# One list reordered: packed attention and an ELU network, with GpSimd's waits for VectorE counted when the list was made

## The chip, the cores and the metric

The kernel runs on one core of a Trainium2 chip. The metric is the time of one execution on the device in microseconds (us), the median of several runs. The engines are named as in the profile: PE is TensorE (matmuls; PEld its weight loads), DVE is VectorE, ACT is ScalarE, POOL is GpSimd, SP is SyncE, which issues the DMAs.

## The reference

Eight batches of eight heads; the queries, keys and values have 576 positions of 64 elements, and there are 32 packing queries `p` for each head. All is float32.

```python
def sm_attn(qq, kk, vv):                 # scale = 1/8
    s = scale * np.matmul(qq, kk.transpose(0, 1, 3, 2))
    s = s - np.max(s, axis=-1, keepdims=True)
    a = np.exp(s)
    a = a / (np.sum(a, axis=-1, keepdims=True) + 1e-09)
    return np.matmul(a, vv)
p_packed = sm_attn(p, k, v)
out = sm_attn(q, p_packed, p_packed)     # [8, 8, 576, 64]
x = out.transpose(0, 2, 1, 3).reshape(4608, 512)
h = x @ w_in                             # [4608, 2048]
g = np.where(h > 0.0, h, np.exp(np.minimum(h, 0.0)) - 1.0)
return g @ w_out                         # [4608, 512]
```

## The kernel before

**Attention.** For each batch the packing attention gives `ppT`, 32 packed rows for each head. The second attention's weights `a` are a [256, 576] matrix for the batch (8 heads times 32 packs, in two groups of 128), made on DVE by transposes, reductions and subtractions (lines 900 to 948) and one exponential on ACT. `ppT` times `w_in` gives a matrix `m`, so that `h` is `a` times `m` over 256 rows (line 1272, in the first two batches 1543).

**Precision.** A matmul runs on parts: each operand is split into a high part (a cast on ACT, line 434) and a low part (word minus high part, on DVE or POOL), and three products (high by high, high by low, low by high) are summed in PSUM.

**The hidden layer.** Its 16 tiles of 128 columns are taken one after the other. In the first two batches each tile goes through two ACT instructions (1561, 1567), the ELU on DVE (1570), the cast (434), the low part `sub_own` (1585, DVE or POOL) and the output matmuls (1658 to 1661). From batch 2 on two tiles go together through a seven-product scheme: after the ELU (1279) three sums of blocks, of 128, 256 and 128 columns, are made in place in a tile `w8` (or `kvq`, for the 64 leftover rows of several batches), each on POOL or on DVE (1354); then one cast of 896 columns on ACT (`hi`, 434), one subtraction on DVE (`lo`, 1362), and 42 matmuls into four PSUM banks (1426). At the end of a visit (16 tiles of one batch) DVE adds the four banks up (1458), and the next visit's matmuls wait for these banks.

**The order.** No scheduler decides it. Some 3,400 operations are recorded, each with the engines it may run on; then the string `ORDER` is read, number by number, and each operation is emitted. A letter behind a number (V, A, G) names DVE, ACT or POOL; without one the first engine of the operation's list is used. `PLACES` gives the PSUM bank of each operation that takes one, `ONES` the matmuls on ones that are put behind some operations at the start. Each engine runs its own instructions in the order emitted, and so does SP's DMA queue.

**GpSimd and VectorE.** Operations that read two tensors of SBUF, and casts and scalings there, are marked `two`. When one of them is emitted on POOL, it gets a wait for the last `two` operation that was emitted on DVE, whether it uses its data or not:

```python
if o.two and e in ("DVE", "POOL"):
    made = nc.cur_bb.bb.instructions[at:]
    if e == "DVE":
        last_two = made[-1]
    elif last_two is not None:
        tc.add_manual_dep(made[0], last_two.name, ...)
```

So the place of a POOL operation in `ORDER`, not its data alone, says when it may start.

Of the kernel before, what the change touches and what calls it, by code (L numbers as in the profile page):

```python
# [25 lines left out]
2 1 7 0 8 9 11 416 417A 418 403 404A 405 10 14 12 3 4 406V 407G 15A 16V 17 18A 19A 20 21 13 23V 408  # L26
22V 409V 410 24 25A 5 26 27 28 29 400 401A 30 402 529 530A 31 424 32 33 34 6 37 425A 426 419 48 55
49 50 420A 755 756 762 757 38 763 421 35A 764 758 39 765 759A 422V 766A 56 40 41 531 57 42 532A 769
43 760G 761 59 411 412A 413 58 62 440 441A 442 767G 60 65 61 414A 63A 64A 432 433V 434 36 770 771
772 776 66A 67A 533 534 773A 44 51 777 778 52 68 69A 415G 535 435 436A 774G 783 784 45 768 70A 71  # L30
779 780V 785 72A 423V 781V 790 427 786 787V 437 438V 428A 429 557 791 792 793 788G 551 552 553 775
558 456 457A 430A 53 439V 801 802 803 458 559 431G 73 74 75 794A 795G 809 76 443 444A 448 810 449A
804 811 445 446A 450 447G 812 805 77 814 782 789 78 554 79 80 560 555 561 562 806A 818 826 54 95
807G 796 815A 816G 81 808 46A 817 459 460A 47 556 819 820 821 822 827 797A 536 828 829 84 82A 461
799A 83 831 823A 451 835 843 452A 453 824G 825 813 85 86 87 832A 462A 833G 834 537 836 837 839 538
830 838 102 844 88 845 848 463G 846 89 90 91 840A 841G 849A 850V 92 852 472 473A 454A 455G 853 854
855 96 856 504 860 861 862 865 863 842 851 93A 94 97 103 857A 491 858V 866A 867V 505A 474 873 880
874 875 492A 506 876 877A 104 878V 859 493 881 800 882 883 887 105 847 499 868 864 884V 500V 885V
888 889 894 890 895 896 897 399 891A 892V 98 501 494A 483 879 464 901 908 798 898A 899V 495V 886 893
902 903 904 475 484A 485 465A 466 909 910 905A 906V 911 502A 503V 871A 915 916 106 917 918 467 900  # L40
922 912A 907 913G 468A 919V 933 486A 469 920V 487V 914 872 923 921 924 925 488 476A 470A 477 478V
496 934 935 937 936 480 926V 489A 515 927V 941 950 107 938A 479V 939V 490 942 943 946 928 940 951
952 954 523 944 953 497A 498 947A 955A 948G 481A 109 958 482 967 956G 959 960 961 945 471G 520 963
968 949 964V 969 516A 970 971 965G 929A 975 507 976 111 957 977 517 978 980 521A 931A 522 972A 981V
973V 984 524A 518A 962 982V 525 985 519V 526V 986 987 563 564 988 992 993 994 508A 565 979 995 966
974 983 989A 997 998A 509 1001 1009 999V 512 112 513A 566 990V 514 991 510A 511V 110 1000 527G 528
1002 643V 932 1003 644V 1005 1004 1006V 1022 567 1010 1011 1012 1014 568 1015A 1016V 1029 996 869A
1007G 1008 1017 113 99 1023 1024 1030 1031 645V 1025 1026V 646A 649V 654A 1032 1033A 652V 653V 655V
930 1034V 108 870 545 569 1018A 1019 1027V 1042 1049 546 547 1020A 1043 1050 1051 1044 1028 650G
# [24 lines left out]
585 1340 586 1326 1327 1328 1350V 1377 1351G 1362 1354 1355 1363 1364 1341 1352 1365V 1366V 1367V
1368 163 1353 1369 1378 1379 1380 1342 1343 1393 1394 1381V 1382G 1395 1396 1397V 1344 1357 1398G
1358 1359 1356 1360 1383V 1384 1399V 1385 1400 1401 1409 1432 1410 1411 1433 165 1434 146 1370 1371
1373 1374 1375 166 167 1412 168 1372 1386 1376 161 169V 1435 1437 1438 1413G 1439 1414G 1415V 1416
1436 1442 1387 1389 1390 1440 1388 1402 1455 170A 1460 1443V 171 1456 1457 1417 1444V 1391 1459 1458
1392 1405 172V 1461 1478 1403 1404 1418 147 148 1462 1463 1465 1445G 1296 1446 1447 173 174 1441 175
176 1479 1483 1480 1481 1406 1484 1466G 1482 1407 1485 1488 1486 177 178 179 1408 1421 1293 1425A  # L80
1489V 195 1467G 1468G 1469 1464 1419 1420 1448 1449 1501 1506 1502 1470 1426 1507 1422 1423 1424
1451 1503 1505 1508 1504 1509 1511 1524 1487 1490G 1491G 1529 1427 1428 1429 196 1492 1493 184 1525
1510 1430 1530 1452 1450 1453 1454 1531 1474 1471 1512G 1513V 1526 1527 1532 1528 1534 180 181 185
1514G 1472 1515 1516 1535G 1536G 1537G 1547 1548 1549 1475 1473 1494 1495 1550 1552 1553 1554 1551
1476 1477 1497 1496 186 187 1557 1533 1555 1570 1538 1571 1539 1558G 1559G 1517 1518 1519 1540 1560G
1572 1574 587 588 589 1575 1576 1577 1573 1578 1498 1499 1580 1500 188 189 1579 1556 190 191 1520
1521 202 1593 1541 1598 1581G 1522 1523 192 1561 1594 1595 1596 1582G 1583G 182A 1562 183 1597 1543
590 1544 1542 1599 1600 1603 1431 1545 1546 1563 1584 193A 591 1601 1564 1566 194 1585 1623 1628 592
1567 1624 1625 1626 1629 1630 1604V 1605V 1606V 1627 1607 593 594 1631 1565 1568 1569 1646 1586 1589
1602 1633 1634G 1635G 1608 1647 1648 1649 595 1587 1651 1652 1653 1650 1590 1588 1609 1591 197 1592  # L90
1656 1657V 1658G 1610 203 206 1632 1611 1639 1654 1640 1641 207 210 204 1636G 1637 208 1638 211 1612
209 1613 1616A 1617 1618 1619 1662 1663 1614 1659G 198 1669 1670 1671 1672 1674 1675 1615 1664 1685
1686 205 1655 1620 1621 1622 1676 1677 1678 1660 1673 1679 212 199 1661 1642 1643 1680V 1644 1645
215 213 1692 1693 1697 216 1665 1681G 1682V 1666 1667 1694 217 218 1698 1695 1683 1696 1699 1702
1687 1700 214 1684 1708 1715 1709 1703G 1716 1717 1720 1701 219 1704V 1705V 1718 596 1668 1688 1721
# [108 lines left out]
ONES = {0: 3, 8: 10, 17: 2, 21: 3, 24: 2, 26: 13, 529: 5}  # L204
# [1606 lines left out]
```

## Time and profile before

| | us |
|---|---|
| three runs, median (lowest, highest) | 686.59 (686.38, 689.18) |
| the profiled execution, its own time | 687.01 |
| its span, first to last instruction | 685.2 |
| PE busy | 642.9 |
| DVE busy | 532.1 |
| ACT busy | 421.1 |
| POOL busy | 173.9 |

The span is one execution as the profiler recorded it; an engine's busy time is the union of its instructions. Matmuls overlap each other in the record, so a busy PE is not a PE at its peak; idle time of PE is time in which it had nothing in flight.

### The profile page before, as it was taken

What the parts mean: (1) busy time and instruction counts of PE and PEld (TensorE: products, weight loads), DVE (VectorE), ACT (ScalarE), POOL (GpSimd) and SP (SyncE); (2) the same over time, 40 slices, a digit from 0 to 9 for tenths busy, and PEclk for the clock granted to TensorE, in tenths of its full rate; (3) what the DMA queues carried; (4) which work ended last, traced back from release to release, by engine and by line L of the source; (5) the groups of instructions that cost most, each with busy time, mean ns of one, the idle gap of its engine ahead of it and who ended that gap; (6) DMA issues with size and microseconds to landing.
All of it is one profiled execution on the core that took longest, in us unless ns stands there. A gap on an engine that the chain in (4) does not pass through costs nothing. (4 is left out here: it accounts for less than half of the span.)

```text
span 685.2 us, 16414 instructions
## 1 busy us (share of the span) xinstructions
PE 642.9 (94%) x6125; PEld 565.0 (82%) x6125; DVE 532.1 (78%) x1068; ACT 421.1 (61%) x804; POOL 173.9 (25%) x275
## 2 busy tenths in 40 slices
PE   8898999998999899999999889998999999999995
PEld 3567987787789788888999788988788888999895
DVE  3998998686998788768888688777877788558465
ACT  3687996555777577645676477645465656445341
POOL 1133023523232242122322232221122322221420
PEclk9999999999999999999999999999999999999998
DMA  9966775654689769887589778877794765574562
GB/s 341 363 219 219 281 208 169 216 170 158 214 277 313 232 212 308 270 286 272 173 264 332 217 235 287 284 247 235 231 345 130 227 211 170 169 228 146 177 194 77
DMA packets 103711, 159.41 MB, mean 233 GB/s; under 512 B 26192, under 2 KB 43088, under 8 KB 103504
## 3 DMA queue, kind: packets, MB, share of 16 engines
q1 hardware_dynamic: 103344, 157.84, 70.7%
q8 instruction: 48, 0.79, 0.5%
q10 hardware_dynamic: 288, 0.52, 0.2%
q14 instruction: 31, 0.25, 0.1%
HBM read 131.85 MB, written 26.48 MB: 231 GB/s over the span
## 5 line engine op out<-in xcount | busy, mean ns | idle before, releaser
L1354 POOL TENSOR_TENSOR w<-w 128x128 f32<-128x128 f32 (+1 forms) x178 | 103.1, 581 | 304.7 <-DVE g L1362 96.4
L434 ACT CAST g<-w 128x896 fp32r<-128x896 f32 x96 | 89.7, 939 | 103.9 <-POOL w L1354 79.2
L1426 PE MATMUL psum<-sw,g 128*128 128x256 f32 x1008 | 150.8, 277 | 1.5 <-DVE part L1458 1.5
L1362 DVE TENSOR_TENSOR g<-w,g 128x896 fp32r<-128x896 f32 x96 | 104.9, 1095 | 47.7 <-ACT g L434 47.0
L1426 PEld LDWEIGHTS psum<-sw,g 128*128 128x128 f32 x1008 | 131.4, 192 | 7.3 <-issue 3.5
L1272 PE MATMUL psum<-a_hi,m_hi 128*128 128x256 f32 (+1 forms) x384 | 113.5, 296 | 9.7 <-DVE w L1279 5.9
L1272 PE MATMUL psum<-a_lo,m_hi 128*128 128x256 f32 (+1 forms) x384 | 110.7, 288 | 0.4 <-DVE a_lo L948 0.4
L1272 PE MATMUL psum<-a_hi,m_lo 128*128 128x256 f32 (+1 forms) x384 | 110.6, 288 | 0.0
L1426 PE MATMUL psum<-wo_a,g 128*128 128x256 f32 x672 | 95.8, 279 | 9.1 <-DVE part L1458 5.1
L1426 PE MATMUL psum<-wo_b,g 128*128 128x256 f32 x672 | 95.6, 277 | 2.1 <-DVE g L1362 2.0
L1426 PEld LDWEIGHTS psum<-wo_a,g 128*128 128x128 f32 x672 | 85.0, 193 | 15.0 <-ACT e L1287 3.4
L1426 PEld LDWEIGHTS psum<-wo_b,g 128*128 128x128 f32 x672 | 84.7, 192 | 6.7 <-issue 3.5
L1272 PEld LDWEIGHTS psum<-a_hi,m_hi 128*128 128x128 f32 x384 | 73.5, 191 | 19.2 <-issue 7.2
L1272 PEld LDWEIGHTS psum<-a_lo,m_hi 128*128 128x128 f32 x384 | 73.6, 192 | 0.6 <-DVE a_lo L948 0.6
L1272 PEld LDWEIGHTS psum<-a_hi,m_lo 128*128 128x128 f32 x384 | 73.5, 191 | 0.0
L1284 ACT ACTIVATE e<-psum 128x320 f32<-128x320 f32 x96 | 41.1, 432 | 33.6 <-PE psum L1272 29.5
L1287 ACT ACTIVATE e<-e 128x320 f32<-128x320 f32 x96 | 44.5, 470 | 2.5
L1354 DVE TENSOR_TENSOR w<-w 128x128 f32<-128x128 f32 (+1 forms) x110 | 37.6, 346 | 9.5 <-POOL w L1354 7.3
L1279 DVE SCALAR_TENSOR_TENSOR w<-e,psum 128x256 f32<-128x256 f32 x96 | 38.7, 415 | 7.5 <-ACT e L1287 6.7
L1024 DVE TENSOR_TENSOR m_lo<-psum,m_hi 128x1024 fp32r<-128x1024 f32 (+1 forms) x38 | 38.7, 1022 | 2.8 <-ACT m_hi L434 2.5
L1279 DVE SCALAR_TENSOR_TENSOR w<-w,psum 128x512 f32<-128x512 f32 x48 | 32.6, 681 | 10.4 <-ACT w L1287 9.6
L1284 ACT ACTIVATE w<-psum 128x512 f32<-128x512 f32 x48 | 28.6, 597 | 19.0 <-PE psum L1272 10.2
(135 smaller groups left out, 1160.4 us busy)
## 6 DMA issues: line engine op xcount, KB each, us to landing
sw<-sw_dram SPq DMA_DIRECT2D x288, 256.0 KB, 4.2
kvq<-in_v SPq DMA_DIRECT2D x16, 512.0 KB, 4.5
raw<-in_w_in SPq DMA_DIRECT2D x16, 511.8 KB, 5.6
raw<-in_w_out SPq DMA_DIRECT2D x16, 511.8 KB, 5.5
kvq<-in_kT SPq DMA_DIRECT2D x14, 576.0 KB, 5.5
kvq<-in_qT SPq DMA_DIRECT2D x14, 576.0 KB, 6.0
out<-part SPq DMA_DIRECT2D x28, 256.0 KB, 4.2
sw_dram<-sw SPq DMA_DIRECT2D x24, 256.0 KB, 2.7
```

The lines of the kernel that those rows point to most:

```text
L434: (nc.scalar.copy if e == "ACT" else nc.vector.tensor_copy)(out=out, in_=in_)
L1024: nc.vector.tensor_tensor(out=m_b[1].t[:, :, fs], in0=ps.t[:, :, :w], in1=m_b[0].t[:, :, fs].bitcast(F32), op=ALU.subtract,)
L1272: nc.tensor.matmul(ps, lhsT=m_b[p].t[:, g, o:o + P], rhs=in_turn(st.a.t[q][:, g, cols]), start=(n == 0), stop=(n == 3 * G - 1),)
L1279: nc.vector.scalar_tensor_tensor(out=out, in0=e_, scalar=-1.0, in1=ps, op0=ALU.add, op1=ALU.max)
L1284: nc.scalar.activation(out=out, in_=ps, func=AF.Relu, scale=-1.0)
L1287: nc.scalar.activation(out=x, in_=x, func=AF.Exp, scale=-1.0)
L1354: eng(e).tensor_tensor(out=out, in0=x, in1=y, op=o)
L1362: nc.vector.tensor_tensor(out=g_b.all[:, 7 * P:(7 + b1 - b0) * P], in0=blocks(b0, b1), in1=g_b.all[:, :(b1 - b0) * P].bitcast(F32), op=ALU ...
L1426: nc.tensor.matmul(a.t[:, at * H:(at + rhs.shape[1]) * H], lhsT=operand(blk, p), rhs=rhs, start=new and n == k == 0, stop=a.final == (u, m ...
```

## The change

The recorded operations are the same, with the same code. `ORDER`, `PLACES` and `ONES` are new: every operation may stand in another place, on another of its engines and in another bank. Line numbers are one lower after the change. The rule of waits above is unchanged. Of the diff two pairs of lines stand here: the place in `ORDER` around operation 841, a `sub_own`, and `ONES`.

```diff
--- before.py
+++ after.py
-830 838 102 844 88 845 848 463G 846 89 90 91 840A 841G 849A 850V 92 852 472 473A 454A 455G 853 854
+838 839 88 89 843 844 845 846 847 453 825 848 834 505A 840A 849V 841V 90 91 850V 454A 455G 852 853
...
-ONES = {0: 3, 8: 10, 17: 2, 21: 3, 24: 2, 26: 13, 529: 5}
+ONES = {0: 3, 8: 8, 17: 2, 21: 6, 24: 2, 26: 13, 529: 4, 37: 1}
```

Counted over the whole list, 32 of the 141 short block sums on POOL and 4 of the 64 long ones go to DVE, and 5 of 30 `sub_own`; 6 casts of `g`, 5 high parts of weights and two of `a` go from ACT to DVE; a few weight operations change in both directions. POOL has 268 instructions of the list before and 230 after, DVE 1,066 and 1,120, ACT 786 and 770.

**First place.** VectorE before, in the second batch; `sm2` and `tmp` belong to a softmax (L922 to L942), `e`, `hb` and `g` to the hidden layer.

```order
L1570 SCALAR_TENSOR_TENSOR e_826<-e_826,psum_101 128x256 [waits Activation_49,Pool_49]
L1570 SCALAR_TENSOR_TENSOR hb_823<-e_826,psum_101 128x64
L922 TENSOR_REDUCE sm2_833<-tmp_758 128x18 [waits DVE_49]
L925 TENSOR_SCALAR sm2_833<-sm2_833 128x18 [waits DVE_49]
L928 RECIPROCAL sm2_833<-sm2_833 128x18 [waits DVE_49]
L931 TENSOR_TENSOR tmp_758<-tmp_758,sm2_833 128x576 [waits DVE_49]
L1585 TENSOR_TENSOR g_841<-e_826,g_841 128x256 [waits Activation_49]
L942 STREAM_TRANSPOSE tmp_844<-tmp_758 128x576 [waits DVE_49]
```

Operation 841 (`g_838<-e_817`) is not in these rows: it stands on POOL and, by its place in the list, waits for the row L931.

VectorE after, same place; the tiles `g_838` and `e_817` are now numbered `g_849` and `e_812`.

```order
L921 TENSOR_REDUCE sm2_820<-tmp_741 128x18 [waits Activation_49]
L1569 SCALAR_TENSOR_TENSOR hb_816<-e_828,psum_101 128x64 [waits Activation_49]
L482 SCALAR_TENSOR_TENSOR mi_833<-raw_681,tops_120 128x512 [waits DMAHW1_49]
L1569 SCALAR_TENSOR_TENSOR e_828<-e_828,psum_101 128x256
L433 CAST g_851<-e_828 128x256 [waits DVE_49,PE_49]
L1584 TENSOR_TENSOR g_849<-e_812,g_849 128x256 [waits Activation_49]
L924 TENSOR_SCALAR sm2_820<-sm2_820 128x18
L927 RECIPROCAL sm2_820<-sm2_820 128x18 [waits DVE_49]
L930 TENSOR_TENSOR tmp_741<-tmp_741,sm2_820 128x576 [waits DVE_49]
L1584 TENSOR_TENSOR g_851<-e_828,g_851 128x256
```

Operation 841 is now on DVE (`g_849<-e_812`) and stands ahead of the softmax's rows L924 to L930.

**Second place.** GpSimd before, some 229 us into the run; each `w8` tile gets three block sums, here those of two pairs that follow each other.

```order
L1354 TENSOR_TENSOR w8_2981<-w8_2981 128x128 [waits DVE_49,Activation_49]
L1354 TENSOR_TENSOR w8_2981<-w8_2981 128x256 [waits DVE_49,Pool_49]
L1354 TENSOR_TENSOR w8_2981<-w8_2981 128x128 [waits Pool_49]
L1354 TENSOR_TENSOR w8_3055<-w8_3055 128x256 [waits DVE_49]
L1354 TENSOR_TENSOR w8_3055<-w8_3055 128x128 [waits Pool_49]
```

The second sum of `w8_2981` has a wait for DVE.

VectorE before, same place; `sm2` and `tmp` are a softmax's, `hb` and `w8` rows L1279 are ELUs, L1362 is `lo`, L1458 adds up the banks of a visit that has ended.

```order
L1279 SCALAR_TENSOR_TENSOR hb_3044<-e_3035,psum_101 128x64 [waits DMAHW0_49,Activation_49]
L1279 SCALAR_TENSOR_TENSOR w8_3055<-e_3035,psum_101 128x256
L1279 SCALAR_TENSOR_TENSOR w8_3055<-e_3052,psum_101 128x256 [waits Activation_49]
L1279 SCALAR_TENSOR_TENSOR hb_3044<-e_3052,psum_101 128x64
L922 TENSOR_REDUCE sm2_3067<-tmp_3021 128x18 [waits Activation_49]
L925 TENSOR_SCALAR sm2_3067<-sm2_3067 128x18 [waits DVE_49]
L928 RECIPROCAL sm2_3067<-sm2_3067 128x18 [waits DVE_49]
L1354 TENSOR_TENSOR w8_3055<-w8_3055 128x128
L1362 TENSOR_TENSOR g_3087<-w8_2981,g_3087 128x896 [waits PE_49,Activation_49]
L1458 TENSOR_TENSOR part_85<-part_85,psum_101 128x256 [waits DMAHW7_49,PE_49]
```

That wait is for the row L1354 of `w8_3055`, a sum of the next pair, which stands behind seven other rows, none of them of `w8_2981`.

GpSimd after; `w8_2981` is now `w8_2995`, `w8_3055` is `w8_3098`.

```order
L1353 TENSOR_TENSOR w8_2995<-w8_2995 128x128 [waits DVE_49]
L1353 TENSOR_TENSOR w8_2995<-w8_2995 128x256 [waits Pool_49]
L1353 TENSOR_TENSOR w8_2995<-w8_2995 128x128 [waits DVE_49,Pool_49]
L1353 TENSOR_TENSOR w8_3098<-w8_3098 128x128 [waits DVE_49]
L1353 TENSOR_TENSOR w8_3098<-w8_3098 128x256 [waits DVE_49,Pool_49]
```

The second sum has no wait for DVE left, and the next pair's first sum is now on POOL as well.

VectorE after, from the ELUs of `w8_2995` on.

```order
L1361 TENSOR_TENSOR g_2969<-w8_2886,g_2969 128x896 [waits PE_49,Activation_49]
L1278 SCALAR_TENSOR_TENSOR w8_2995<-e_2986,psum_101 128x256 [waits DVE_49,Activation_49]
L1278 SCALAR_TENSOR_TENSOR hb_3000<-e_2986,psum_101 128x64 [waits DMAHW2_49]
L1278 SCALAR_TENSOR_TENSOR w8_2995<-e_3002,psum_101 128x256 [waits Activation_49]
L1278 SCALAR_TENSOR_TENSOR hb_3000<-e_3002,psum_101 128x64
L899 STREAM_TRANSPOSE tmp_3017<-psum_101 128x576 [waits DMAHW5_49,DMAHW4_49,DMAHW6_49,DMAHW3_49,PE_49]
L908 TENSOR_REDUCE mx2_3039<-tmp_3017 128x18 [waits DVE_49]
L911 TENSOR_TENSOR tmp_3017<-tmp_3017,mx2_3039 128x576 [waits DVE_49]
L1361 TENSOR_TENSOR g_3012<-w8_2946,g_3012 128x896 [waits Activation_49]
L1278 SCALAR_TENSOR_TENSOR hb_3095<-e_3047,psum_101 128x64 [waits DMAHW0_49,Activation_49]
```

The first sum's wait is for the last ELU row of `w8_2995` (L1278), and no sum of the next pair stands between the two.

## Rows read from the trace of the kernel before

**Rows 1.** The page, part 1: span; busy time, share, instructions of each engine.

```profile
span 685.2 us, 16414 instructions
...
PE 642.9 (94%) x6125; PEld 565.0 (82%) x6125; DVE 532.1 (78%) x1068; ACT 421.1 (61%) x804; POOL 173.9 (25%) x275
```

**Rows 2.** PE waits: who ended them, us in total, times, longest.

```profile
PE psum L1426 <- DVE part L1458: 6.6, 6, 2.0
PE psum L1272 <- DVE w L1279: 5.9, 6, 2.4
PE psum L1661 <- POOL g L1585: 5.0, 4, 1.8
...
PE psum L1536 <- ACT m_hi L434: 2.0, 1, 2.0
```

**Rows 3.** Waits of the other engines, same columns.

```profile
POOL w L1354 <- DVE g L1362: 96.4, 35, 8.1
ACT g L434 <- POOL w L1354: 79.2, 38, 5.5
...
DVE g L1362 <- ACT g L434: 60.7, 52, 2.9
POOL w L1354 <- DVE w L1354: 50.0, 25, 8.0
```

**Rows 4.** Timeline 60 to 65.2: start, us, instruction; idle before, its releaser.

```profile
62.73 0.76 DVE L931 TENSOR_TENSOR tmp<-tmp,sm 128x576 f32<-128x576 f32 x1
...
63.65 0.75 POOL L1585 TENSOR_TENSOR g<-e,g 128x256 fp32r<-128x256 f32 x1 [2.45 <-DVE tmp L931]
...
64.46 0.70 PE L1661 MATMUL psum<-wo_a,g 128*128 128x512 f32 x2 [1.75 <-POOL g L1585]
```

**Rows 5.** Timeline 226 to 234.5, same columns.

```profile
229.11 0.23 DVE L1354 TENSOR_TENSOR w<-w 128x128 f32<-128x128 f32 x1
...
229.48 1.26 POOL L1354 TENSOR_TENSOR w<-w 128x256 f32<-128x256 f32 x2 [1.79 <-DVE w L1354]
...
230.78 0.94 ACT L434 CAST g<-w 128x896 fp32r<-128x896 f32 x1 [2.39 <-POOL w L1354]
...
231.75 1.09 DVE L1362 TENSOR_TENSOR g<-w,g 128x896 fp32r<-128x896 f32 x1 [2.41 <-ACT g L434]
...
232.76 0.41 DVE L1458 TENSOR_TENSOR part<-part,psum 128x256 f32<-128x256 f32 x1
...
233.32 0.91 PE L1426 MATMUL psum<-wo_a,g 128*128 128x256 f32 x6 [2.03 <-DVE part L1458]
```

**Rows 6.** Timeline 672 to 674.5, PE alone.

```profile
673.26 0.71 PE L1426 MATMUL psum<-wo_b,g 128*128 128x256 f32 x4 [0.42 <-DVE g L1362]
```

**Rows 7.** Groups by form: busy us, mean ns; idle before, its releasers.

```profile
L1354 POOL TENSOR_TENSOR w<-w 128x128 f32<-128x128 f32 x121 | 58.5, 485 | 234.2 <-DVE g L1362 73.3 <-DVE w L1279 72.8 <-DVE w L1354 30.5
...
L1354 DVE TENSOR_TENSOR w<-w 128x128 f32<-128x128 f32 x71 | 20.9, 298 | 3.7 <-POOL w L1354 2.1
...
L1354 DVE TENSOR_TENSOR w<-w 128x256 f32<-128x256 f32 x39 | 16.9, 432 | 5.7 <-POOL w L1354 5.2
...
L1585 DVE TENSOR_TENSOR g<-e,g 128x256 fp32r<-128x256 f32 x34 | 14.1, 430 | 1.3 <-ACT g L434 1.2
...
L434 DVE CAST g<-e 128x256 fp32r<-128x256 f32 x15 | 5.4, 369 | 0.8
```

**Rows 8.** Stretches of 50 us: PE, PEld, DVE, ACT, POOL busy; clock; DMA.

```profile
50.00:100.00 50.00, 48.25 (x337) 41.59 (x337) 45.08 (x99) 43.51 (x96) 10.80 (x13) 1.00 0.69 229
...
150.00:200.00 50.00, 47.27 (x354) 38.76 (x353) 43.13 (x96) 32.75 (x76) 14.92 (x20) 1.00 0.63 210
```

**Rows 9.** Source line L1354 on DVE: duration ns min/median/max.

```profile
L1354 DVE TENSOR_TENSOR w<-w x110: 228/293/840, 193.2 to 670.1; 128x128 f32<-128x128 f32 x71, 128x256 f32<-128x256 f32 x39
```

**Rows 10.** Two stretches at a PE gap, columns as in Rows 8.

```profile
546.00:550.00 4.00, 2.02 (x18) 1.86 (x17) 3.29 (x8) 3.11 (x6) 0.73 (x1) 1.00 0.18 65
550.00:553.00 3.00, 3.00 (x17) 3.00 (x17) 2.90 (x6) 0.91 (x2) 0.00 (x0) 0.61 0.10 22
```

More of the change, by code (lines that the diff above doesn't have):

```diff
@@ L194 @@
[L194 to L195 removed]
+2 1 7 0 8 9 10 11 403 404V 12 405 406V 407V 3 14 15A 16A 17 4 416 417V 418 400 5 20 18A 19A 13 21
+401V 22A 23A 408 24 424 402 25A 26 27 28 29 6 48 55 49 409A 410 529 30 530A 425A 419 31 32 33 34 37
+50 426 35A 755 38 39 36 756 757 758 40 762 763 764 765 56 420A 421 759A 766V 760G 57 531 59 41 767V
+532A 769 58 776 411 62 412V 60 65 413 422A 61 414V 432 761 433A 434 415V 440 441A 442 770 777 771
@@ new lines @@
+977 524A 980 978 979 525 981V 966 521A 522 985 986 982V 987 988 508A 992 993 994 509 510V 512 995
+997 974 989A 990V 526A 929V 527V 998A 999V 1001 1009 1002 1003 1005 511V 98 99 996 1004 513A 1010
+1011 514 528 1012 983 991 112 1006A 1007V 643V 1014 1022 930 1023 1024 113 931A 932 566 567 1000
+1008 644V 645V 1015A 1016V 646A 1025 1026A 568 114 1029 647V 649V 654A 652V 1027V 1030 1031 653V
+1017 1018A 1042 650V 1028 655V 656 1020A 1021 1032 1033A 545 657V 658G 569 1043 1044 1045 1046A 1049
+1056 546 547 1034G 1035 1047G 570 571 572 1050 115 659V 1051 1052 1057 666V 667V 1053A 573 1063
@@ new lines @@
+1309 1310 746 1318V 1319G 157 155 140A 141 145 146 158 1330 1331 1332 1320 1321 1311 159 1333V 1334G
+160 1324 1338 1346 1312 1335G 1347 1339 1340 1361 162 164 1348 1354 163 1325 1326 1327 1328 1336
+1337 1377 165 1349G 1350G 1351G 585 586 1362 1363 1364 1365V 1352 1355 1356 1370 1341 1342 1343
+1366V 166 1367V 1368 1353 167 1393 1344 1357 1371 1358 1359 1360 1378 1379 1369 1373 1380 1381G
+1382V 1293 1383V 1394 1296 1395 1396 1384 1385 1372 1386 1397G 1409 1387 1388 168 1410 1411 1432
+1374 1433 1375 1402 1398V 1399G 1412 1413V 161 170V 1400 1401 1414V 1434 1435 147 148 195 1437 1403
@@ new lines @@
+1376 1438 169A 1436 1389 1439 1442 1440 1441 1443V 171 172A 1415V 1390 1416 1417 1404 1455 1460 1456
+1457 1391 1459 1392 1458 1461 1418 1419 1462 1465 1444G 1445G 1446 1463 1420 173 1405 1448 1449
+1466G 1467G 174 175 1478 1479 1483 196 1406 176 1468G 1447 177 1407 184 1408 1484 1421 1464 1480
+1481 1485 1482 1488 1489G 1469 1486 1487 178 1501 179 1450 1470 1502 1503 1506 1507 180 1504 1505
+1490G 1422 1508 197 1423 1509 1425A 1510 1426 1427 1491G 1511 1471 1472 1424 1492 1428 1429 1430
+1524 1525 1512G 1513G 1493 1451 1529 1452 1530 1531 1473 1494 1495 1526 1528 1527 1534 1514G 1453
@@ new lines @@
+614 2321 2307 2263 2291 2322 2323 2326 2327 2309G 2268V 2269 2270 2271 2310G 2311G 324 2290 2292
+2293 325 2314 2325 2324 2328 2329 2330 615 618 2331 2344 2332V 2333G 616 617 2312 2313 2349 2267
+2294 2345 2346 2348 2315 2347 2316 2350 2351 2354 2295 2337 2338 2367 2352 2353 2272 2372 2334V 619
+2273 620 2296 2297 2317 2318 2368 2355G 2356G 2357G 319 2369 2370 2373 2374 2335 2336 2371 2377
+2378V 2339 2360 2361 2375 2376 326 327A 2379V 2380V 2358 2359 2390 2391 2392 2395 2319 2320 2340
+2362 2394 328V 329 2396 2397 2393 2398 2400 2401V 2413 305 306 2381 2382 2399 2414 2415 2416 2417
@@ new lines @@
+638 2983 2962G 2963V 2981 2931 2932 2984V 2953G 2933 2993 2894 2895 639 2896 2916 2920A 2934 2935
+2949 2966 2954 2917 3006 3007 3008 2918 2919 2985G 640 2982 2921 2922 2923 641 3011 3012 2936 2924
+2955 2925 3013 2926 3009 3014 3015 2937 2938 2939 2964 3010 3016 3017V 2986V 2987 3039 2967 2968
+2999 3040 3041 3044 3045 3046 642 2988 3042 3043 2956 2957 2965 2958 2959 3047 3018G 2994G 3049
+2995V 2996V 3050G 3051G 2969 2970 2971 3000 2972 2989 3026 3027V 3028V 3001 3048 3072 2997 3019V
+3020 2998 3032 3033 2990 2991 3021 3059 3029V 3073 3074 3076 3075 3060G 2992 3002 3003 3004 3052V
```

313 lines of the change are left out of this document (139 added, 174 removed).

## Prediction

> **What bounds the kernel now.** I read the page's first part, then who ended PE's waits, then the waits of the other engines, and then the timeline backwards from PE's gaps. PE has something in flight for 642.9 of 685.2 us [rows 1], so a gain has to come out of the other 42.3 us, apart from small lateness that hides in the overlap of matmuls. No engine but PE is full: DVE is busy for 532.1 us, POOL for 173.9.
>
> PE's largest waits end with a DVE addition that frees a bank (6.6 us), an ELU that frees a bank (5.9), and POOL's low part of `g` (5.0) [rows 2]. What makes these late is seen one engine further back. ACT's cast of 896 columns waits 79.2 us for sums on POOL, DVE's `lo` 60.7 us for that cast, and POOL's sums wait 96.4 us for `lo` and 50.0 us for a sum on DVE [rows 3]. A sum on POOL takes 0.485 us as a mean [rows 7]; the waits are several times the work.
>
> Two places show how that reaches PE. At 64.46 PE stands still for 1.75 us for a low part on POOL; that POOL instruction sat idle for 2.45 us until a softmax multiplication on DVE (0.76 us long) was under way to its end [rows 4]. It uses nothing of the softmax: this is the wait which the place in the list gives it. At 229.48 POOL's second and third sum of a pair wait 1.79 us for a sum of another pair on DVE (0.23 us); the cast starts at 230.78, `lo` at 231.75, and behind `lo`, in DVE's queue, the addition at 232.76, for which PE waits 2.03 us [rows 5].
>
> I followed every PE gap back in this way. In 26 of them, the first at 64.46 [rows 4] and the last, of 0.42 us, at 673.26 [rows 6], the way back through DVE and ACT meets a POOL instruction that had itself been idle for a DVE instruction. Their idle time adds up to 20.8 us, half of the 42.3. The other half is the start, the end, and gaps that DVE's queue makes alone.
>
> **The change, part by part.** *POOL's waits.* For each block sum on POOL I counted the DVE work that the two orders put between the last instruction whose result the sum needs and the one that it must wait for, with durations from the trace before. More than 1.5 us of foreign work stands there for 78 of 205 sums before and 22 of 169 after. For the POOL instructions of the 26 gaps the new order has either DVE as their engine (15 of them, operation 841 of the first place among them) or at most 0.6 us of foreign work (9, the second place among them); the two left, with three gaps of 3.3 us together, keep 1.9 and 5.9 us of it. So 20.8 - 3.3 = 17.5 us can go. Of these, PE's direct waits for POOL, 5.0 us in 4 gaps [rows 2], have nothing behind POOL, and I take them whole. The other 12.5 us pass through DVE's queue, where the next late thing is whatever else is queued. The ends are 0 and 12.5; the second place, where 1.79 of 2.03 us would go [rows 5], is near the upper end, stretches in which DVE is busy for 45.08 of 50 us [rows 8] near the lower; I take half, 6.2. Together -11.2 us (ends 0 and -17.5).
>
> *More work on DVE.* DVE gets 54 instructions more. From row means: 32 short sums by 0.298, 4 long by 0.432, 5 low parts by 0.430, 6 casts by 0.369 [rows 7] are 9.5 + 1.7 + 2.2 + 2.2 = 15.6 us; the remaining exchange of weight, `a` and evacuation work comes to about 2.3 us by the same kind of row, so 17.9 us in all. It is hidden while DVE has idle time and nothing of PE's is queued behind; the cover is PE's 642.9 against 532.1 us. It is not hidden where DVE is nearly full: two of the 14 stretches of 50 us have DVE at 45.08 and 43.13 us [rows 8], 100 of 685 us. I take that share, 0.15 of 17.9, +2.7 us; the ends are 0 and +17.9. ACT loses 16 and POOL 38 instructions; neither is near its limit, so 0. In a few places POOL instructions still wait long; queued behind them are only POOL's own next sums, whose casts wait for them.
>
> *Collisions.* A sum on DVE takes 0.293 us as the median, and once 0.840 [rows 9]; the long ones lie next to POOL instructions. The Trainium skill (SBUF — State Buffer, "Who interferes with whom") says that a DVE instruction with two SBUF inputs and a GpSimd instruction that reads SBUF exclude each other, and that the one that issues second blocks until the first is done. The longest row agrees with it. By that rule also the two-input DVE instruction that the list puts right behind a POOL one would pay, 129 such neighbours before and 87 after; at half of a POOL sum, an estimate of 0.24 us each, DVE would get 10 us back, and the +2.7 would be +1.2.
>
> *The start.* PE waits 2.0 us for a cast to `m_hi` at 28 us [rows 2]. After the change a cast of `g` is off ACT's queue ahead of it, and the softmax step that this queue waits for stands ahead of two others on DVE. I take -0.7 us, ends -2.0 and +2.0. The 39 matmuls on ones in place of 38 lie in PE's waits: 0.
>
> *Banks and DMAs.* Every bank is chosen anew, and SP's queue is in another order. None of PE's long waits ends with a DMA [rows 2], so I take 0 for the queue; for the banks 0, with an upper end that is a rival below.
>
> The profiled execution took 687.0 us, 0.4 more than the median. 687.0 - 11.2 + 2.7 - 0.7 = 677.8, and against the median some 677.5 us.
>
> **The rivals.** *DVE's queue takes back the rest.* Only the direct waits go: 687.0 - 5.0 + 2.7 - 0.7 - 0.4 = 683.6 us, no change that can be told. For it speaks that DVE's ELUs and additions stand between POOL and PE in 22 of the 26 gaps; against it, that DVE itself waits 60.7 us for the cast [rows 3] and so has room. The Trainium skill (Perfetto Trace Analysis, "Optimizing Scalar/DVE Operations") says that moving work between GpSimd and DVE might not help, since they share a read port; by that rule it would be this case.
>
> *New banks.* A bank that is taken again sooner makes PE wait for the ELU or the addition that reads it. These two waits are 5.9 and 6.6 us now [rows 2]; if they doubled, 677.4 + 12.5 = 689.9 us, at the edge of what can be told. Against it speaks that both are queue waits, which come from late `lo`s as at 229 us.
>
> *DVE becomes the bound.* This one is slower: all 17.9 us land on PE's path, 687.0 - 11.2 - 0.7 + 17.9 - 0.4 = 692.6 us. It decides from the point where (11.2 + 0.7 + 3.4) / 17.9, or 85%, of the added work is on the path. Against it: DVE would be at about 550 of 680 us.
>
> *The clock.* After the gap at 547 to 549 us the granted clock is 0.61 of full speed between 550 and 553 [rows 10], that is partly at 1.2 in place of 2.4 GHz; this costs about 0.39 x 3 = 1.2 us beside the gap. Each long gap that the new order makes or removes can carry such a sum. It is inside the range.
>
> **How the numbers follow.** Chances: the forecast 0.70, DVE's queue 0.15, new banks 0.07, DVE as the bound 0.08. The range begins where all 17.5 us go and DVE's work is free, 687.0 - 17.5 - 0.7 - 0.4 = 668.4, say 668; it ends at 687, which holds the first rival and leaves out the two at 690 and above and little else. A difference under 0.5% (3.4 us) can't be told from none here. Faster by more than that (below 683.2 us): the forecast, 0.70. The same: the first rival and most of the second, 0.20. Slower (above 690.0): the last and the rest of the second, 0.10.
>
> **What would show it.** Right: PE's idle time falls from 42 to about 33 us; the waits of ACT's cast for POOL from 79.2 to under 50 us; PE's direct wait for POOL's low part from 5.0 to under 2 us; DVE's busy time rises to some 550 us and POOL's falls to some 155. The two places have no PE gap over 0.5 us. Wrong: the ACT and POOL waits fall but PE's waits for DVE's ELUs and additions (12.5 us now) grow as much, or PE's gaps turn up in places where there were none. The forecast fails most easily in the half that I took for DVE's queue, and in new gaps that no row of the old order can show.

## The result, and the profile after

| | before | after |
|---|---|---|
| median of runs, us (lowest, highest) | 686.49 (686.21, 689.18), 4 runs | 647.69 (646.39, 649.16), 4 runs |
| ratio, with its 95% interval | | 0.9427 (0.9393, 0.9461) |
| profiled execution, its span | 685.2 | 647.4 |

The change saves 38.8 us. The forecast was 9 us, and the result lies below its range. The direction was right, the size was not.

The page of after, part 1, beside [rows 1]:

```profile
span 647.4 us, 16383 instructions
...
PE 631.1 (97%) x6123; PEld 561.0 (87%) x6126; DVE 540.3 (83%) x1122; ACT 416.7 (64%) x788; POOL 152.4 (24%) x237
```

PE's idle time falls from 685.2 - 642.9 = 42.3 us to 647.4 - 631.1 = 16.3 us. That is 26.0 of the 37.8 us of span. The other 11.8 us come out of PE's busy time. The mean granted clock rose from 0.991 to 0.998, which is about 0.007 x 685 = 4.8 us. That the 7 us left lie between matmuls that overlap in the record and yet start later than they could is likely, but no row here shows it.

PE's waits of after, beside [rows 2] (who ended them, us in total, times, longest):

```profile
PE psum L888 <- DMA kvq<-in_qT: 2.1, 2, 1.1
PE psum L1271 <- DVE w L1278: 1.8, 1, 1.8
PE psum L827 <- DMA tmp<-turn_dram: 1.5, 2, 1.1
...
PE psum L1535 <- ACT m_hi L433: 1.2, 1, 1.2
```

The addition that frees a bank (6.6 us) and POOL's low part (5.0) are gone from the list, the ELU has 1.8 left of 5.9, and two DMAs are among the longest waits now, with 3.6 us together (a third has 1.0).

Waits of the other engines in after, beside [rows 3], same columns:

```profile
POOL w L1353 <- DVE w L1353: 102.6, 28, 8.0
POOL w L1353 <- DVE g L1361: 74.8, 19, 11.9
...
ACT g L433 <- POOL w L1353: 36.8, 29, 4.5
...
DVE g L1361 <- ACT g L433: 22.7, 22, 4.2
```

POOL waits for DVE no less than before (the two rows have 177.4 us, 146.4 in [rows 3]); POOL's idle time by itself says nothing, only who waits for POOL does. What fell is the cast's wait for POOL, by 42.4 us, and `lo`'s wait for the cast, by 38.0.

Where in the run the time came from is read from the first and the last start of one PE line (source lines, duration ns min/median/max, first and last start). Before, the first start of L1272, in batch 2, and the last of L1426:

```profile
L1272 PE MATMUL psum<-a_hi,m_hi x384: 272/299/474, 184.9 to 663.5; 128*128 128x256 f32 x96, 128*128 128x320 f32 x96
...
L1426 PE MATMUL psum<-sw,g x1008: 272/275/422, 198.6 to 678.0; 128*128 128x256 f32 x168
```

After:

```profile
L1271 PE MATMUL psum<-a_hi,m_hi x384: 272/299/403, 181.9 to 631.9; 128*128 128x256 f32 x96, 128*128 128x320 f32 x96
...
L1425 PE MATMUL psum<-sw,g x1008: 272/275/377, 191.9 to 641.5; 128*128 128x256 f32 x168
```

3.0 us are gained by the first start, 36.5 by the last: 33.5 us come between the two, in batches 2 to 7, where three sums on POOL or DVE stand ahead of each cast.

### The profile page after: what moved, and what is told of

Same layout as the page of the kernel before. It is cut to its first block, busy times and chain, and to the rows that moved or that the text cites. A ratio compares the mean times of both kernels' runs of the same rounds, so it can differ in the third digit from the quotient of the medians.

```text
span 647.4 us, 16383 instructions
## 1 busy us (share of the span) xinstructions
PE 631.1 (97%) x6123; PEld 561.0 (87%) x6126; DVE 540.3 (83%) x1122; ACT 416.7 (64%) x788; POOL 152.4 (24%) x237
## 4 chain that ended last, share of the span: by engine, by line
PE 82%; DMA 8%; DVE 5%; ACT 2%; issue 1%; SPq 1%; DVEq 0%; ACTq 0%
PE psum L1425 38%; PE psum L1271 20%; PE psum L1542 5%; PE psum L1010 4%; PE psum L1657 3%; PE psum L1658 3%; PE psum L1660 3%; DMA kvq<-in_qT 2%; DMA sw<-sw_dram 2%; DMA tmp<-turn_dram 2%; PE psum L827 1%; PE psum L888 1%; DMA raw<-in_w_in 1%; PE psum L1535 1%; DMA part_dram<-part 1%
## 5 line engine op out<-in xcount | busy, mean ns | idle before, releaser
L1353 POOL TENSOR_TENSOR w<-w 128x128 f32<-128x128 f32 (+1 forms) x150 | 85.6, 573 | 309.9 <-DVE w L1353 102.6
L1425 PE MATMUL psum<-sw,g 128*128 128x256 f32 x1008 | 150.8, 276 | 1.0 <-DMA sw<-sw_dram 1.0
L1425 PEld LDWEIGHTS psum<-sw,g 128*128 128x128 f32 x1008 | 131.1, 192 | 9.2 <-issue 5.2
L433 ACT CAST g<-w 128x896 fp32r<-128x896 f32 x96 | 90.1, 939 | 74.9 <-POOL w L1353 36.8
L1271 PE MATMUL psum<-a_hi,m_hi 128*128 128x256 f32 (+1 forms) x384 | 111.9, 291 | 1.8 <-DVE w L1278 1.8
L1271 PE MATMUL psum<-a_lo,m_hi 128*128 128x256 f32 (+1 forms) x384 | 110.2, 287 | 0.0
L1271 PE MATMUL psum<-a_hi,m_lo 128*128 128x256 f32 (+1 forms) x384 | 110.2, 287 | 0.0
L1425 PE MATMUL psum<-wo_b,g 128*128 128x256 f32 x672 | 94.0, 276 | 0.0
L1425 PE MATMUL psum<-wo_a,g 128*128 128x256 f32 x672 | 93.7, 276 | 0.0
L1425 PEld LDWEIGHTS psum<-wo_b,g 128*128 128x128 f32 x672 | 84.2, 192 | 3.6 <-issue 3.6
L1425 PEld LDWEIGHTS psum<-wo_a,g 128*128 128x128 f32 x672 | 84.3, 192 | 1.7 <-issue 0.8
L1271 PEld LDWEIGHTS psum<-a_hi,m_hi 128*128 128x128 f32 x384 | 73.2, 191 | 6.2 <-issue 4.2
L1271 PEld LDWEIGHTS psum<-a_lo,m_hi 128*128 128x128 f32 x384 | 73.3, 191 | 0.0
L1271 PEld LDWEIGHTS psum<-a_hi,m_lo 128*128 128x128 f32 x384 | 73.2, 190 | 0.0
L1353 DVE TENSOR_TENSOR w<-w 128x128 f32<-128x128 f32 (+1 forms) x138 | 44.9, 332 | 8.9 <-POOL w L1353 6.7
L1278 DVE SCALAR_TENSOR_TENSOR w<-e,psum 128x256 f32<-128x256 f32 x96 | 38.5, 415 | 11.7 <-ACT e L1286 10.7
L1560 ACT ACTIVATE e<-psum 128x256 f32<-128x256 f32 (+1 forms) x64 | 26.0, 409 | 23.3 <-PE psum L1542 14.7
```

The costliest lines, as they stand in the source:

```text
L433: (nc.scalar.copy if e == "ACT" else nc.vector.tensor_copy)(out=out, in_=in_)
L1271: nc.tensor.matmul(ps, lhsT=m_b[p].t[:, g, o:o + P], rhs=in_turn(st.a.t[q][:, g, cols]), start=(n == 0), stop=(n == 3 * G - 1),)
L1278: nc.vector.scalar_tensor_tensor(out=out, in0=e_, scalar=-1.0, in1=ps, op0=ALU.add, op1=ALU.max)
L1353: eng(e).tensor_tensor(out=out, in0=x, in1=y, op=o)
L1425: nc.tensor.matmul(a.t[:, at * H:(at + rhs.shape[1]) * H], lhsT=operand(blk, p), rhs=rhs, start=new and n == k == 0, stop=a.final == (u, m ...
L1560: nc.scalar.activation(out=pairs(e_b.t[:, :n_tok]), in_=h(slice(0, n_tok)), func=AF.Relu, scale=-1.0)
```

## The experiments

Run beside the experiments, the kernel before took 687.5 to 688.6 us (medians); the ratios, and the gains of single experiments, are against these. "Holds" means POOL's waits, by the added rule, for DVE work that it has no use for. Where only `ORDER` changes, the diff shows a fragment of it.

**The change taken apart: engines alone (e1), places and banks alone (e2).**

```diff
 e1, in before.py
-1438 1413G 1439 1414G 1415V 1416
+1438 1413V 1439 1414V 1415V 1416
 e2, in after.py
-840A 849V 841V 90 91
+840A 849A 841G 90 91
```

273 operations have another engine after the change; e1 gives them that engine at their old places and banks, e2 takes it from them at their new ones. The counts in the section on the change are what is left when both directions are set off: of the block sums and `sub_own`, 111 go from POOL to DVE and 70 from DVE to POOL (41 is the difference); of the other 92, 45 go from ACT to DVE, 29 back, 8 from POOL to DVE and 10 back.

> The old list with its places and banks, but every operation on the engine that the new list gives it. Theory A (a POOL instruction held for foreign DVE work delays the cast, the cast holds DVE's queue at lo, and all that stands behind lo is late; taking those holds away gives back most of the 38.8 us): the moved sums lose their holds, the 169 that stay on POOL keep theirs, so part of the gain, 662 to 675 us. Theory B (the gain is the engines: less work on POOL, where a sum takes 0.485 us against 0.298 on DVE): nearly all of it, 647 to 655 us. Theory C (the new arrangement of all queues and banks is what helps, the POOL holds being worth about the 11 us of the forecast): 680 to 690 us.

> The new list and banks, but every operation on the engine of the old list. Theory A: the places are what removes the holds, but the 41 operations sent back to POOL stand in places that were not made for them, 650 to 665 us. Theory B: the gain goes, 678 us or more. Theory C: most of it stays, 650 to 660 us.

e1 took 718.4 us (ratio 1.0445, interval 1.0417 to 1.0473), slower than any theory had it; e2 took 674.3 us (0.9811, 0.9786 to 0.9835), between the ranges of A and B. Alone, the new engines cost 30 us and the new places save 14; together they save 39. The two can't be costed one by one and added up, as the forecast did. `lo`'s wait for the cast, in e1 and then in e2:

```profile
DVE g L1362 <- ACT g L434: 62.1, 52, 3.4
```

```profile
DVE g L1361 <- ACT g L433: 29.9, 30, 2.3
```

e2's first and last starts, as above, show what its 14 us hide:

```profile
L1271 PE MATMUL psum<-a_hi,m_hi x384: 273/299/634, 193.3 to 656.2; 128*128 128x256 f32 x96, 128*128 128x320 f32 x96
...
L1425 PE MATMUL psum<-sw,g x1008: 272/275/378, 204.9 to 665.8; 128*128 128x256 f32 x168
```

Up to batch 2 it is 8.4 us later than before (193.3 and 184.9 us), and behind that it gains 20.6 of the change's 33.5 us.

**The holds made short (e3), or taken away (e4), in the old list with the old engines and banks.** e3 writes each block sum and each `sub_own` on POOL directly behind the last operation whose result it uses; 1414 is the second sum on POOL of its tile. e4 drops the added wait and moves nothing.

```diff
 e3
-167 1412 168 1372 1386 1376 161 169V 1435 1437 1438 1413G 1439 1414G 1415V
+167 1412 1413G 1414G 168 1372 1386 1376 161 169V 1435 1437 1438 1439 1415V
 e4
                 elif last_two is not None:
-                    tc.add_manual_dep(made[0], last_two.name, ...)
+                    pass
```

> The old list, engines and banks, with one thing changed: each block sum and each low part of g that runs on POOL stands right behind the last operation that it needs, so that the DVE instruction it must wait for is one of its own inputs or an older one. No other queue changes. Theory A: PE's gaps go, 648 to 662 us, and DVE's wait for the cast falls from 60.7 to under 30 us. Theory B: no gain, 680 us or more. Theory C: the forecast's share alone, 673 to 680 us.

> The old list, engines and banks, without the added wait: POOL waits for its data alone. Theory A: as the run with POOL early, 648 to 662 us, unless the two engines then hold each other up at their shared port; then DVE's two-input instructions lengthen (a sum over 0.293 us, lo over 1.09 us as the median) and the time is above that. Theory B: 680 us or more. Theory C: 673 to 680 us.

e3 took 652.1 us (0.9488, 0.9461 to 0.9516), e4 648.8 us (0.9433, 0.9417 to 0.9449). Without one engine or bank chosen anew, they gain 35.9 and 39.1 us, the change 38.8. The waits of e4:

```profile
PE psum L1272 <- DVE hb L1279: 1.5, 2, 1.3
...
ACT g L434 <- POOL w L1354: 21.2, 19, 2.6
...
DVE g L1362 <- ACT g L434: 22.9, 32, 2.7
```

`lo`'s wait for the cast falls to 22.9 us, as in the change (22.7), and with it go nearly all of the PE waits for ELUs and additions that stand behind `lo` in DVE's queue. The gain comes in the same part of the run as the change's: 4.3 us by the first start, 37.3 by the last.

```profile
L1272 PE MATMUL psum<-a_hi,m_hi x384: 272/299/403, 180.6 to 628.8; 128*128 128x256 f32 x96, 128*128 128x320 f32 x96
...
L1426 PE MATMUL psum<-sw,g x1008: 272/275/377, 193.5 to 640.7; 128*128 128x256 f32 x168
```

Groups of e4 by form (busy us, mean ns):

```profile
L1354 POOL TENSOR_TENSOR w<-w 128x128 f32<-128x128 f32 x121 | 72.3, 600 | 194.1 <-DVE w L1279 138.5 <-DVE w L1354 39.9 <-ACT w L1287 4.6
```

What the added wait keeps away shows too: the sum on POOL takes 600 ns in place of 485 [rows 7], POOL is busy for 201.2 us in place of 173.9, DVE for 543.8 in place of 532.1. In this list the wait keeps some 39 us of busy time off two engines that have room, and costs some 39 us of the kernel's time; nothing makes these two numbers equal.

**Which holds: the block sums (e7) or the low parts (e8), each alone.** The edits are e3's for one kind:

```diff
 e7
-167 1412 168 ... 1438 1413G 1439 1414G 1415V
+167 1412 1413G 1414G 168 ... 1438 1439 1415V
 e8
-427 786 787V 437 438V 428A ... 791 792 793 788G 551
+427 786 787V 788G 437 438V 428A ... 791 792 793 551
```

> Old list, engines and banks; only the block sums on POOL are written directly behind the last operation whose result they use, the low parts sub_own stay where they were. Theory A (sum late, cast late, lo late, and DVE's queue behind lo late): most of the 36 us that both hoists gave together, 655 to 665 us; DVE's wait of lo for the cast falls from 60.7 to about 30 us, PE's direct wait for POOL's low part stays near 5 us. Rival, the forecast's way of counting (only half of what passes through DVE's queue comes back): 678 to 684 us.

> Old list, engines and banks; only the 30 low parts sub_own on POOL are written directly behind the last operation whose result they use, the block sums stay. Theory A: sub_own stands only in the first two batches and nothing but PE waits for it, so only the direct wait of 5.0 us and what follows from it goes: 679 to 684 us, DVE's wait of lo for the cast stays near 60 us. Rival (the low parts are where the gain came from): 655 to 668 us.

e7 took 655.4 us (0.9533, 0.9496 to 0.9570), e8 685.5 us (0.9990, 0.9963 to 1.0017), which can't be told from no change and is 1.5 us above theory A's range. The block sums carry it, although PE never waits for one directly. e7 keeps exactly the direct wait that the forecast took whole, and loses the one that it halved:

```profile
DVE g L1362 <- ACT g L434: 27.3, 36, 2.7
...
ACT g L434 <- POOL w L1354: 21.1, 19, 3.4
...
PE psum L1661 <- POOL g L1585: 5.0, 4, 1.8
```

e8 takes 3.3 of these 5.0 us away, and the kernel is no faster for it:

```profile
PE psum L1660 <- POOL g L1584: 1.7, 1, 1.7
...
DVE g L1361 <- ACT g L433: 61.2, 51, 2.9
```

**Does the new list need its waits (e5, e6)?** e5 is the change with e4's edit. e6 keeps the wait for the first 500 operations:

```diff
-                elif last_two is not None:
+                elif last_two is not None and len(seen) <= 500:
```

> The list, engines and banks of the change; only the added wait of GpSimd for VectorE's last two-tensor operation is taken out, as in the run of the old list without it (648.8 us). Theory A (the holds for foreign work are what cost time, and the new list has lost nearly all of that cost): little is left to gain, 643 to 648 us; ACT's wait of the cast for POOL falls from 36.8 to about 20 us, DVE's wait of lo for the cast stays near 22 us. Rival (the new list is good for another reason, and its holds still cost what the old ones did): 610 to 630 us. Second rival (the wait keeps collisions away, and with DVE fuller than before the new list needs it): 652 to 665 us, PE waiting for DVE.

> The list, engines and banks of the change; the added wait of GpSimd for VectorE is kept for the first 500 operations of the list (about 97 us) and left out behind them. Without any added wait this list took 656.5 us, and matmul by matmul it fell 5.7 us behind between 19 and 97 us, where VectorE has no idle time, and nothing behind that. Theory C (collisions at the port cost time only where VectorE is full): the whole loss comes back, 645 to 649 us, and PE's starts follow those of the change within 1 us up to 97 us. Rival (the loss is spread over the run, or the waits help elsewhere): 652 to 657 us.

e5 took 656.5 us (0.9542, 0.9514 to 0.9570), 9 us more than the change (8 by the ratios); e6 took 650.2 us (0.9446, 0.9411 to 0.9482), whose interval covers the change's ratio; it lies between the two ranges that were named for it. For e5 the second rival had the time right against theory A, but not its sign: PE's idle time is 18.7 us, 16.3 in the change.

e4 and e5 together say what the change's gain is made of. With the added wait the old list takes 686.5 us and the new one 647.7; without it they take 648.8 and 656.5. Where the wait is gone the new list gains nothing, and it gains nothing over e4 either where the wait is kept for the first 500 operations alone (e6, 650.2). So all of the change's gain is time that this wait cost the old list.

What e5 loses against the change is read from the stretch of 40 to 97 us (columns as in [rows 8]), in after and then in e5:

```profile
40.00:97.00 57.00, 55.28 (x408) 45.40 (x401) 53.62 (x121) 48.92 (x103) 14.11 (x15) 1.00 0.74 240
```

```profile
40.00:97.00 57.00, 53.28 (x390) 41.20 (x388) 55.04 (x110) 45.86 (x97) 15.35 (x14) 1.00 0.71 229
```

DVE has hardly an idle moment there, and without the wait it does 110 instructions where it did 121. A full DVE is not enough for such a loss: in e4 it is as full in the old list, and the first L1272 comes no later than before (180.6 us, 184.9 before).

```profile
40.00:97.00 57.00, 55.62 (x402) 45.09 (x400) 54.74 (x111) 49.07 (x108) 17.04 (x17) 1.00 0.71 237
```

One of e5's instructions, from its timeline (start, us, instruction), DVE and then POOL:

```profile
42.11 1.76 DVE L482 SCALAR_TENSOR_TENSOR w_in_sb<-raw,tops 128x512 uint32<-128x512 uint32 x1
...
42.02 1.30 POOL L496 TENSOR_TENSOR wo_a<-mi,wo_a 128x512 fp32r<-128x512 f32 x1 [0.67 <-ACT wo_a L433]
```

In after the same instruction takes 0.68 us:

```profile
41.36 0.68 DVE L482 SCALAR_TENSOR_TENSOR w_in_sb<-raw,tops 128x512 uint32<-128x512 uint32 x1
```

It started 0.09 us behind POOL's and took 1.08 us longer; POOL's had 1.21 us to go. So far as one row can, this agrees with the rule of the Trainium skill (SBUF — State Buffer, "Who interferes with whom") that the second to issue is blocked until the first is done. The first L1271 in e5, and then in e6:

```profile
L1271 PE MATMUL psum<-a_hi,m_hi x384: 272/299/404, 187.2 to 638.0; 128*128 128x256 f32 x96, 128*128 128x320 f32 x96
```

```profile
L1271 PE MATMUL psum<-a_hi,m_hi x384: 272/299/474, 181.4 to 636.4; 128*128 128x256 f32 x96, 128*128 128x320 f32 x96
```

After the change it starts at 181.9; the last L1425 starts at 647.6, 646.0 and 641.5. So 5.3 of the 6.1 us that e5 loses are lost up to batch 2, and these go away with the wait there. e6's profile is of an execution that took 653.7 us, 3.5 more than its median, so what it loses later (some 5 us) stays open.

**Earlier still, in the new list (e9).** e3's edit on the change, wait kept:

```diff
-1503 1506 1507 180 1504 1505 1490G 1422
+1489G 1490G 1491G 1469 ... 1503 1506 1507 180 1504 1505 1422
```

> The list, engines and banks of the change with the added wait kept; only the block sums and low parts on POOL are written directly behind the last operation whose result they use. Theory A, by which the new list has lost nearly all cost of the holds: 645 to 650 us, no difference from the change that can be told; ACT's wait of the cast for POOL falls from 36.8 to about 20 us and PE's idle time stays near 16 us. Rival (holds that are left still cost): 635 to 643 us. Second rival (early POOL work collides with DVE where DVE is full): 651 to 656 us.

e9 took 660.6 us (0.9592, 0.9561 to 0.9624), 13 us more than the change (11 by the ratios); more than any theory had. Its timeline at 600 us, POOL, DVE and PE:

```profile
592.99 0.28 DVE L1353 TENSOR_TENSOR kvq<-kvq 128x128 f32<-128x128 f32 x1
...
598.87 2.46 POOL L1353 TENSOR_TENSOR kvq<-kvq 128x128 f32<-128x128 f32 x4 [10.57 <-DMA kvq<-rest_dram]
...
601.37 0.29 DVE L1353 TENSOR_TENSOR kvq<-kvq 128x128 f32<-128x128 f32 x1 [8.10 <-POOL kvq L1353]
...
602.72 1.22 PE L1425 MATMUL psum<-wo_b,g 128*128 128x256 f32 x4 [5.43 <-DVE g L1361]
```

A sum on leftover rows now heads POOL's queue while its rows are still on their way from memory. Behind it stands a sum of another tile, of which DVE had made the first sum by 593.3 us; DVE waits 8.1 us for it. A place in a queue can hold work up without any added wait. Stretches behind this gap (columns as in [rows 8]):

```profile
602.50:606.00 3.50, 3.28 (x15) 3.28 (x16) 2.87 (x5) 1.94 (x5) 0.00 (x0) 0.50 0.00 0
606.00:610.00 4.00, 4.00 (x31) 4.00 (x30) 3.90 (x10) 1.95 (x3) 1.65 (x3) 0.80 0.16 60
```

The gap and the clock behind it make some 5.4 + 0.5 x 3.5 + 0.2 x 4 = 8 us (an estimate) of the 12.5 by which the last L1425 is late (654.0 us, 641.5 after); the rest was not followed.

**Why the new engines lose at the old places (e10, e12, e13, e14).** e10 is e1 without the added wait; e12 is e10 with those sums and low parts written early, as in e3, that are on POOL under the old or the new choice of engines. e13 and e14 divide e10's 273 switched operations: the 181 sums and low parts, and the 92 others (its text counts 89). All four lack the added wait.

```diff
 e12, against e10
-167 1412 168 1372 1386 1376 161 169A 1435 1437 1438 1413V 1439 1414V 1415V
+167 1412 1413V 1414V 168 1372 1386 1376 161 169A 1435 1437 1438 1439 1415V
 e13, against e4
-89 90 91 840A 841G 849A 850V
+89 90 91 840A 841V 849A 850V
 e14, against e4
-89 90 91 840A 841G 849A 850V
+89 90 91 840A 841G 849V 850V
```

> The list and banks of before with the engines of the change (718.4 us with the added wait), and the added wait taken out. Theory A (the new engines were slow there because the old places hold POOL for still more foreign DVE work): 645 to 660 us, PE idle 15 to 25 us, DVE's wait of lo for the cast under 30 us. Rival (the new engines put too much on DVE at the old places; the in-order queue itself is too long there): 685 to 715 us, with DVE's waits small and PE waiting for DVE rows.

> The old list with the new engines and without the added wait (693.4 us), and beside that each of the 195 or so sums and low parts that are on POOL under either choice of engines is written directly behind the last operation whose result it uses. Theory D (a place in the list holds a sum that has gone to DVE by DVE's own order just as the added wait held it on POOL; the switched sums have 2.5 foreign DVE operations ahead of them at the old places as a mean, 1.1 at the new ones): most of the difference to 648.8 us comes back, 650 to 670 us, DVE's wait of lo for the cast falls from 45.7 to under 30 us. Rival (the load is what is wrong, 54 more instructions on DVE): it stays at 685 to 700 us. Third possibility: DVE, reaching the early sums before POOL has made their neighbours, stands still for POOL; then DVE's wait for POOL grows from 10 to over 25 us.

> The old list and banks without the added wait (648.8 us), and of the new engines only those of the block sums and of sub_own (181 of them change between DVE and POOL, both ways); all else keeps its old engine. With all new engines it took 693.4 us. Theory E (POOL's sums have to come between others of their tile at once; a switch at a place that was chosen for the other engine puts a stall into DVE's in-order queue): most of the 44.6 us is here, 675 to 695 us. Rival (the loss comes from the casts, high and low parts that change between ACT and DVE): 648 to 660 us.

> The old list and banks without the added wait (648.8 us), and of the new engines only those of the operations that are neither block sums nor sub_own (89 casts, high and low parts, normalizations and evacuations); the sums keep their old engines. Theory E: a small part of the 44.6 us, 650 to 665 us, in the first two batches, where most of these operations stand. Rival: 680 to 695 us.

e10 took 693.4 us (1.0074, 1.0042 to 1.0107), e12 701.7 (1.0191, 1.0159 to 1.0222), e13 679.9 (0.9876, 0.9846 to 0.9906), e14 660.7 (0.9601, 0.9575 to 0.9627). The holds were 25 of e1's 718.4 us; of the other 44.5 us above e4, the switched sums alone make 31.1 (e13) and the rest alone 11.9 (e14), together 43.0. e10 lies where its rival had it, but against that rival's sign `lo` still waits 45.7 us for the cast; e13 and e14 lie where theory E had them. The two losses lie in different parts of the run, as first and last starts show (e13, then e14; e4 above):

```profile
L1272 PE MATMUL psum<-a_hi,m_hi x384: 272/299/404, 182.9 to 658.5; 128*128 128x256 f32 x96, 128*128 128x320 f32 x96
...
L1426 PE MATMUL psum<-sw,g x1008: 272/275/422, 197.2 to 672.2; 128*128 128x256 f32 x168
```

```profile
L1272 PE MATMUL psum<-a_hi,m_hi x384: 272/299/404, 192.4 to 642.0; 128*128 128x256 f32 x96, 128*128 128x320 f32 x96
...
L1426 PE MATMUL psum<-sw,g x1008: 272/275/377, 205.9 to 653.9; 128*128 128x256 f32 x168
```

The switched sums lose 2.3 us up to batch 2 and 29.2 behind it, the others 11.8 and 1.4. e13's waits:

```profile
DVE g L1362 <- ACT g L434: 48.2, 49, 3.4
...
ACT g L434 <- POOL w L1354: 43.5, 26, 3.7
ACT g L434 <- DVE w L1354: 40.6, 21, 4.6
```

The cast waits for sums on DVE as long as for POOL's, with no added wait anywhere. e12 shows that it isn't the sum's place alone (theory D fell):

```profile
DVE w L1353 <- POOL w L1353: 19.7, 25, 1.4
DVE g L1361 <- ACT g L433: 19.3, 27, 2.8
DVE kvq L1353 <- POOL kvq L1353: 14.6, 6, 4.9
```

It cuts `lo`'s wait to 19.3 us, but DVE, which reaches early sums before POOL has made their neighbours, then waits 34.3 us for POOL's sums (12.1 in e10), as the third possibility had it, and the time rises. So the switch of engine and the places of its neighbours belong together; which of the switched sums do the harm stays open.

## Why the prediction was wrong, step by step

**The step that failed is the term "POOL's waits"**, -11.2 us with -17.5 as its far end. It took the direct waits whole (5.0 us), halved what passes through DVE's queue (6.2 of 12.5), and left out the "gaps that DVE's queue makes alone". The runs turn this round: early low parts take 3.3 of the 5.0 us of direct waits away and give 2 us that can't be told from nothing (e8); early block sums, the queue part, give 32.1 us (e7); the holds as a whole are worth 39.1 us (e4). DVE's queue was no independent second cause that takes gains back. It was late because `lo`, at its head, waited for a cast that waited for a held sum: `lo`'s wait [rows 3] fell by 37.8 us in e4 and by 38.0 in the change, and the gains were 39.1 and 38.8. The forecast quoted these 60.7 us as room on DVE; in the old list with its engines they were the stall itself. That wait is no price by itself, though: in e2 it fell by 30.8 us for a gain of 14, and in e12 by 41.4 in a run that was slower than before. Following back from PE's gaps, gap by gap, stopped at DVE instructions that were busy by then but late because of an earlier `lo`; that this is how gaps beyond the 26 were missed is argued, not shown by a run. And the bound that the forecast set first, that a gain has to come out of PE's 42.3 idle us, missed 11.8 us of it.

That the change's own gain is this one is shown by e4 and e5: without the added wait the new list has no gain over the old. Its list has the same fall of `lo`'s wait, and a smaller one of the cast's wait for POOL (to 36.8 us, 21.2 in e4). How much of the 39 us its places give and how much its engines isn't settled: the places with the old engines give 14 us (e2), the engines at the old places lose 30 (e1).

**More work on DVE**, +2.7 us: no price of its own shows. DVE's busy time rose by 8.2 us, where the forecast had 17.9; but 17.9 adds up durations, and busy time counts overlapping rows once. With the same engines at the old places it rose by 15.6 (e1). The new places are faster with the new engines than without (e2). In the stretch where DVE is full, less work gets done once collisions come on top (e5). **Collisions:** DVE's longest sum is 496 ns after, 840 before [rows 9]. Without the wait DVE is busy for 11.7 us more in the old list (e4) and 12.0 more in the new (e5), POOL for 27.3 and 13.0; the old list is faster all the same, the new one slower. Neither the +2.7 nor the +1.2 of the forecast can be read off as time.

**The start**, -0.7 us: PE's wait for `m_hi` went from 2.0 to 1.2 us. **Banks**, 0: PE's waits for the instructions that free them shrank, so that rival is out; no run changes the banks alone. **DMAs**, 0: 4.6 us of PE's waits now end with three of them.

**The rivals.** DVE's queue taking back the rest, new banks, and DVE as the bound are all out, as the time fell below the range. That an exchange of work between POOL and DVE might not help, as the first of them has it, fits the old places (e1) and not the new ones. **The clock:** the stretch after the largest gap of an experiment (e9) was granted 0.50, so long gaps do carry such a sum.

**The signs named ahead:** the cast's wait for POOL is under 50 us (36.8), PE's direct wait for POOL's low part is off the list, POOL is at 152.4 us, DVE at 540.3 against some 550; PE's idle time is 16.3 where 33 was named. Neither place has a PE gap left. At the first, operation 841 is done on DVE at 60.77 us, and the matmuls that use it start at 61.98 without a wait (timeline of after):

```profile
60.35 0.42 DVE L1584 TENSOR_TENSOR g<-e,g 128x256 fp32r<-128x256 f32 x1
...
61.98 0.59 PE L1660 MATMUL psum<-wo_a,g 128*128 128x512 f32 x2
```

At the second, one hold is left. The third sum of the tile still waits 0.97 us for a softmax subtraction (L911) that it does not use. The cast starts 1.3 us behind that sum; the last thing that it waited for was PE, not POOL, and `lo` follows it at once:

```profile
220.48 1.18 POOL L1353 TENSOR_TENSOR w<-w 128x128 f32<-128x128 f32 x1 [0.97 <-DVE tmp L911]
...
222.97 0.94 ACT L433 CAST g<-w 128x896 fp32r<-128x896 f32 x1 [0.87 <-PE psum L1425]
...
223.94 1.09 DVE L1361 TENSOR_TENSOR g<-w,g 128x896 fp32r<-128x896 f32 x1
```

## What to carry to other kernels

Price a wait by the waits of the engines that it makes late, up to the last queue in order, and not by the PE gaps that can be traced to it: a long wait at the head of a busy in-order queue may be the stall and not room. One such wait is a sign and not the price (e12 has the shortest and is slower); a run without the cause is. Before a list is reordered around a wait that guards a shared resource, run it once without that wait; the one run tells what the guard costs (here all of the gain). Run the new list without it too: here the guard paid in the one stretch where DVE was full (e5, e6), while the old list lost nothing in that stretch without it. Choose engines and places together: here either alone gave a third of the gain, or a loss.

## What the hardware showed that was not expected

Unguarded overlap of DVE and POOL was cheap for the kernel: a 128x128 sum on POOL took 600 ns where it took 485, and DVE was busy for 2% more (e4), although a single instruction could take 1.76 us in place of 0.68 (e5). After a PE gap of 5.4 us the granted clock was 0.50 of full speed for 3.5 us, that is the lower of the two levels, 1.2 GHz, throughout, and 0.80 in the next 4 us (e9).
